# Scores of one pair issued before waiting transposes, copies of the last pair issued at once, a split last accumulator, and another route for the decoded weights

## The chip, the cores and the metric

One core of one Trainium2 chip. The time of a kernel is the device time of one execution in microseconds (us), the median of several executions.

## The reference

Three stages on 4 x 576 = 2304 tokens of width 512 (8 heads of 64):

```python
scores = 0.125 * q @ k.T                       # per batch and head, 576 x 576
scores = where(causal, -1e9, scores + decay)   # decay: differences of cumsum(log(clip(f, 1e-4, 1)))
x = softmax(scores) @ v                        # heads put side by side: 2304 x 512
h = x @ w_in;  x = (h - tanh(h)) @ w_out       # layer 0: 512 -> 2048 -> 512
h = x @ w_in;  x = (h * sigmoid(h)) @ w_out    # layer 1, other weights
```

q, k, v and f arrive as float32, the four weight matrices as float64. The result is float32.

## The kernel before

**Numbers.** TensorE multiplies in a reduced float32 form, so every operand is kept as a high part and the rest (hi and lo), and a product of two operands is three matmuls: hi x hi, hi x lo, lo x hi. The float64 weights have to be decoded first. A `raw` tile holds two 32-bit words of each of 128 x 1024 weights. `wjob` (L191) takes a weight through these steps: `scale` (ACT, L203) rescales the words with the exponent, `shift` (DVE, L207) moves the high word into a tile `wa`, `exponent` (DVE, L211) puts its exponent bits into `wb`, `low` (DVE, L214) turns the low word into a float in `wb`, `join` (DVE, L226) adds the two into `ws`, `sum` (DVE, L230) forms four more blocks of 256 columns in `ws`, and `HI` (ACT, L247) and `LO` (DVE, L249) make the two parts `wh`, `wl` (and `weh`, `wel`) that TensorE reads. A weight is named (q, m): q counts pairs of 128-wide slices of the hidden width, 8 per layer, and m is 0 for w_in and 1 for w_out.

**Attention (0 to about 178 us).** It goes over 16 pairs of heads, each of nine tiles of scores. For pair p the calls `scores(p, u)`, u = 0 to 3, put matmuls into a tile `s`; DVE takes the row minimum (L1328), ACT the exponential (L1336), POOL divides by the sum (L1350). `transposes(p, u)` then turns the tiles p into PSUM tiles `t` (PE, L1362), of which there are three places, and `evac(p, u)` issues the copies of `t` into `ptf` (ACT or DVE, L1407), from which `values` multiplies with v. A list `due` says at which of the tile steps each call is issued; copies are registered one step after their transposes:

```python
later(n0 + k[u], transposes, p, u)
later(n0 + k[u] + 1, evac, p, u)
```

Within a step transposes come before scores. `pt_0` is the tile of the last 64 queries of pair 0, and turning it waits for POOL's L1350 on it.

**Start of layer 0 (about 165 to 263 us).** The first three units (a unit is one set of weights, 4 slices of the hidden width, times one of three blocks of 768 tokens) run from slots written out by hand (PE L475 and L431, ACT L341, L481, L500, L449, DVE L328, L342, L482, L504).

**The joint stage (263 us to the end).** The other 21 units run with two alternating pieces on PE: `h_step` (L656, twelve matmuls of 384 columns, one of seven block products of the first matrix) and `c_step` (L729, eighteen of 256 columns or twelve of 384, one of seven of the second matrix). The products accumulate in four PSUM banks: two `h` and two `a`. Where a partial sum serves two results, ACT copies one bank into the other ("seed", L944 and L1023). `x` collects the results through DVE additions (`gain`, L1031). The order here is not written by hand: `joint` lists tasks with an engine, a cost in steps, what they read and write and a due time, and `planned` (L1123) lays them out engine by engine; each engine then runs its instructions in that order.

**DMA.** Nearly all transfers are issued by SP, in order. An issue that has to wait holds back all behind it. Per unit SP loads seven `xr` tiles (L625, 768 KB). A partial sum of layer 0 that must wait for the next set is put aside: `aside_store` (L673) writes the tile `aside` to DRAM and `aside_load` (L676) brings an earlier one back into the same tile, so the load waits until the store has landed. Loads of `raw` (L164) follow the `low` step of the weight before:

```python
if what[0] == "low":
    raws.pop((q, m))
    wload(q + 1, m)
```

**The end.** In the last unit the seven products of `c_step` come as 1, 5, 6, 2, 7, 3, 4. Products 1, 6, 2, 7 and the last, 4, add into the bank called y, whose sums are also read by other results before product 4 may write it. After product 4 three DVE additions of 256 columns (L1031, `gain(..., d=d)`) go into `x`, and two stores (L801), on ACT's and SP's queue, end the kernel.

Of the kernel before, what the change touches and what calls it, by code (L numbers as in the profile page):

```python
# [48 lines left out]
def forgetting_attention_two_ffn(  # L49
# [104 lines left out]
    raws, wtiles, wjobs = {}, {}, {}  # L154

    def wload(q, m, parts=(0, 1)):
        if q >= 2 * NPR:
            return
        l, c = divmod(2 * q, NFC)
        if (q, m) not in raws:  # L160
            raws[q, m] = rawp.tile([P, 2, DM, 2], U32, tag=f"raw{m}", name=f"raw{q}_{m}")
        for i in parts:
            to = raws[q, m][:, i].rearrange("p n w -> p (n w)")
            nc.sync.dma_start(out=to, in_=(w_in, w_out)[m][l][c + (i if m and q >= 2 * S0 else 1 - i)])  # L164

# [29 lines left out]
    def wjob(q, m, what, part=None):  # L195
# [5 lines left out]
        if what == "scale":  # L201
            high = rd(raws[q, m][:, i, :, 1])
            nc.scalar.activation(high, high, AF.Prelu, scale=2.0 ** -112, alpha=-(2.0 ** 32))  # L203
        elif what == "shift":
            if "a" not in st:
# [21 lines left out]
        elif what == "sum":  # L227
            s = st["s"]
            to, p, op, r = RECIPE[m * (2 - l)][part]
            nc.vector.tensor_tensor(s[:, to], s[:, p], s[:, r], op)  # L230
        elif what in ("hi", "lo"):
            hi, lo = wtile(q, m)
            frm = st["s"][:, 1:8] if m == 0 else st["w"]
            if m:
                hi, lo = (t.rearrange("p (i k) f -> p i (k f)", i=2) for t in (hi, lo))
            c = i if m else (slice(0, 3), slice(3, 7), slice(7, 8))[part]
            frm = st["s"][:, 0:1] if m == 0 and part == 2 else frm[:, c]
            if what == "hi":
                nc.scalar.copy(hi[:, c], frm)
            else:  # L240
                nc.vector.tensor_tensor(lo[:, c], frm, rd(hi[:, c]), ALU.subtract)
        else:
            for to, n, frm in GROUPS[m and l + 1][part]:
                hi, lo = place(q, to) if m else (w[:, to:] for w in wtile(q, 0))
                hi, lo, frm = hi[:, 0:n], lo[:, 0:n], st["s"][:, frm:frm + n]
# [440 lines left out]
    def cbank(u, i):  # L686
# [23 lines left out]
    def c_step(u, k):  # L710
# [7 lines left out]
        for d in range(3 if l else 2):  # L718
            ds = slice(d * P, d * P + P)
            for j, (wh, wl) in enumerate(ws):  # L720
                gh, gl = (t[:, e, j] for e in range(2))
                if l:
                    dst = acc[:, d // 2, 256 * (d % 2):256 * (d % 2) + 256]
# [60 lines left out]

    def csum(u, t, d=None):
        if units[u][0]:
            t = t.rearrange("p b c -> p (b c)")
            return t[:, 0:TB] if d is None else t[:, 256 * d:256 * d + 256]
        return t[:, :, 0:TH]

# [12 lines left out]
    def joint():  # L803
# [15 lines left out]

        W2, N2, basis = dve(TB), act(TB), {}  # L820
        base = {U0: 0}
# [8 lines left out]
        def decode(q, m):  # L830

            l = 2 * q // NFC
            job, raw = (lambda *a: lambda: fill((q, m) + a)), ("raw", m)
            yield "D", 3.5, None, (), (raw,), None
            yield "A", act(DM * 2), job("scale"), (raw,), (raw,), None
            yield "V", 0.33, job("shift"), (raw,), ("wa",), None
            yield "V", 0.33, job("exponent"), ("wa",), ("wb",), None
            yield "V", dve(1024), job("low"), (raw,), ("wb", raw), None
            if m and q // 2 in PLAINSETS:
# [4 lines left out]
                return  # L844
            yield "V", dve(1024), job("join"), ("wa", "wb"), tuple(("ws", k) for k in range(8)), None
            for k, (to, p, op, r) in enumerate(RECIPE[m * (2 - l)]):
                yield "V", dve(256), job("sum", k), (("ws", p), ("ws", r)), (("ws", to),), None
            groups = [0, 1, 2] if m and q // 2 in MIXED else [0, 1]
            behind = m and l and q % 2 and 3 * (q // 2) - 1 in PLAIN and q // 2 not in MIXED
            for g in [1, 3, 4, 5] if behind else groups:  # L850
                cols, key = [("ws", k) for to, n, f in GROUPS[m and l + 1][g] for k in range(f, f + n)], wkeys(q, m, g)
                yield "A", act(256 * len(cols)), job("HI", g), cols, key, g
                yield "V", dve(256 * len(cols)), job("LO", g), cols + key, key, None

        def spread(t0, t1, jobs, since):
# [3 lines left out]
            for e, c, fn, r, w, tag in jobs:  # L859
                if e == "D":  # L860
                    task(t - 6, e, c, fn, r, w)
                    continue
# [53 lines left out]
        for u in range(U0, len(units) + 1):  # L916
# [93 lines left out]
            for k, i in enumerate(csteps(v)):  # L1010
                if plain_:
# [3 lines left out]
                    continue  # L1015
                kd = ("h", v % 2) if last and i in (5, 3) else kz if i in (2, 3, 5) else ky
                n = gop(v, k)
                r = [kd, ("gh", n % 3), ("gl", n % 3)] + [w for j in range(2) for w in (wkeys(q + j, 1, 1) if WAT[l][i] >= 8 else [("w", (q + j) % NSLOT, 1, 10 + WAT[l][i])])]
                when = t0 + k if last else t0 + 2 * k + 1
                task(when, "P", 1, lambda v=v, k=k: c_step(v, k), r, (kd,))  # L1020
# [4 lines left out]
            def gain(when, c, frm, kf, op=PLUS, copies=False, d=None):  # L1025
                to = xs[c] if d is None else xs[c][:, 256 * d:256 * d + 256]
                if copies:
                    task(when, "A", N2, lambda: copy(to, frm), (kf,), (kx[c],), True)
                else:
                    n = W2 if d is None else dve(256)  # L1030
                    task(when, "V", n, lambda: tt_(to, *((frm, to) if op == PLUS else (to, frm)), op), (kf, kx[c]), (kx[c],), True)  # L1031

# [69 lines left out]
            else:  # L1102
# [11 lines left out]
                send(t0 + 6.6, 12)  # L1114
                for d in range(3):
                    gain(t0 + 7.05 + 0.01 * d, 21, csum(v, y, d), ky, d=d)
                    if d:
                        send(t0 + 7.055 + 0.01 * d, 21, slice(0, 2) if d == 1 else slice(2, 3), (nc.scalar, nc.sync)[d - 1])

# [74 lines left out]
    def attention(first):  # L1194
        with ExitStack() as actx:
# [156 lines left out]
            def transposes(p, u):  # L1352
# [277 lines left out]
```

## Time and profile before

| | us |
|---|---|
| median of 3 runs (lowest to highest) | 901.84 (901.59 to 902.15) |
| profiled execution, its time | 901.59 |
| its span, first to last instruction | 899.8 |
| PE busy (6079 matmuls) | 890.6 (99%) |
| DVE busy | 784.7 (87%) |
| ACT busy | 602.2 (67%) |
| POOL busy, all of it before 178 us | 161.2 (18%) |

The granted clock of TensorE is 0.999 of full speed over the span. Rows of the timeline give the start and length of an instruction (or of a run of equal ones, "x4") and, in square brackets, how long its engine stood idle ahead of it and what ended that. Rows of the chain of waits give a start, a length and the engine and line that stood on the path that ended last. "L" is a line of the kernel.

### The profile page before, as it was taken

What the parts mean: (1) busy time and instruction counts of PE and PEld (TensorE: products, weight loads), DVE (VectorE), ACT (ScalarE), POOL (GpSimd) and SP (SyncE); (2) the same over time, 40 slices, a digit from 0 to 9 for tenths busy, and PEclk for the clock granted to TensorE, in tenths of its full rate; (3) what the DMA queues carried; (4) which work ended last, traced back from release to release, by engine and by line L of the source; (5) the groups of instructions that cost most, each with busy time, mean ns of one, the idle gap of its engine ahead of it and who ended that gap; (6) DMA issues with size and microseconds to landing.
All of it is one profiled execution on the core that took longest, in us unless ns stands there. A gap on an engine that the chain in (4) does not pass through costs nothing.

```text
span 899.8 us, 16280 instructions
## 1 busy us (share of the span) xinstructions
PE 890.6 (99%) x6079; PEld 846.1 (94%) x6079; DVE 784.7 (87%) x1321; ACT 602.2 (67%) x1006; POOL 161.2 (18%) x242
## 2 busy tenths in 40 slices
PE   9999999999999999999999999999999999999997
PEld 7777777799999999999999999999999999999997
DVE  7799999798889999998999999997997799776647
ACT  6888888765556666766676678866765666555443
POOL 8999999400000000000000000000000000000000
PEclk9999999999999999999999999999999999999999
DMA  5434533467458677787678665777767566555753
GB/s 166 157 97 149 177 122 97 190 249 279 192 224 304 247 262 245 248 295 273 226 273 290 211 241 202 274 273 266 246 236 264 201 225 231 192 186 179 235 166 123
DMA packets 51103, 196.04 MB, mean 218 GB/s; under 512 B 9744, under 2 KB 15120, under 8 KB 50992
## 3 DMA queue, kind: packets, MB, share of 16 engines
q1 hardware_dynamic: 50744, 194.72, 61.7%
q8 instruction: 48, 0.79, 0.3%
q14 instruction: 31, 0.25, 0.1%
q10 hardware_dynamic: 280, 0.28, 0.1%
HBM read 151.98 MB, written 41.88 MB: 215 GB/s over the span
## 4 chain that ended last, share of the span: by engine, by line
PE 96%; DVE 1%; ACT 1%; POOL 1%; issue 0%; DVEq 0%; POOLq 0%; ACTq 0%
PE h L656 34%; PE a L729 32%; PE a L431 5%; PE t L1362 5%; PE s L1315 5%; PE out_t L1418 5%; PE h L475 4%; PE a L761 2%; PE s L1307 2%; PE h L461 2%; PE out_t L1446 1%; PE out L1418 0%; DVE x L1031 0%; DVE gr L988 0%; PE h L729 0%
## 5 line engine op out<-in xcount | busy, mean ns | idle before, releaser
L656 PE MATMUL h<-xr,wh 128*128 128x384 f32 x1176 | 299.3, 335 | 0.1
L656 PEld LDWEIGHTS h<-xr,wh 128*128 128x128 f32 x1176 | 208.8, 188 | 0.5 <-ACT h L944 0.4
L656 PE MATMUL h<-xr,wl 128*128 128x384 f32 x588 | 196.8, 335 | 0.0
L656 PEld LDWEIGHTS h<-xr,wl 128*128 128x128 f32 x588 | 110.4, 188 | 0.0
L987 ACT CAST gr<-f 128x768 fp32r<-128x768 f32 x104 | 86.8, 838 | 32.5 <-PE a L729 29.9
L988 DVE TENSOR_TENSOR gr<-f,gr 128x768 fp32r<-128x768 f32 x104 | 98.7, 952 | 3.9 <-ACT gr L987 3.9
L729 PE MATMUL a<-wh,gr 128*128 128x256 f32 x516 | 99.2, 282 | 0.0
L1336 ACT ACTIVATE p<-p,mn 128x128 f32<-128x128 f32 (+3 forms) x128 | 71.3, 559 | 18.0 <-DVE mn L1328 15.3
L729 PEld LDWEIGHTS a<-wh,gr 128*128 128x128 f32 x516 | 83.0, 191 | 0.0
L1031 DVE TENSOR_TENSOR x<-a,x 128x768 f32<-128x768 f32 (+1 forms) x64 | 59.3, 929 | 21.4 <-PE a L729 21.1
L729 PE MATMUL a<-weh,gr 128*128 128x256 f32 x384 | 74.1, 283 | 0.3 <-DVE x L1031 0.3
L1350 POOL TENSOR_SCALAR p<-p,sm 128x128 f32<-128x128 f32 (+3 forms) x128 | 72.6, 582 | 7.5 <-DVE sm L1347 6.9
L729 PE MATMUL a<-gr,wh 128*128 128x384 f32 x288 | 73.4, 335 | 0.4 <-DVE gr L988 0.4
L729 PE MATMUL a<-wl,gr 128*128 128x256 f32 x258 | 72.9, 283 | 0.0
L1023 ACT COPY a<-a 128x768 f32<-128x768 f32 x49 | 38.4, 783 | 49.4 <-PE a L729 46.8
L1328 DVE CUSTOM_DVE_ANT_0 p<-s,mask 128x128 f32<-128x128 f32 (+3 forms) x128 | 59.6, 479 | 13.1 <-PE s L1315 13.1
L729 PEld LDWEIGHTS a<-weh,gr 128*128 128x128 f32 x384 | 61.8, 191 | 0.7 <-issue 0.5
L944 ACT COPY h<-h 128x768 f32<-128x768 f32 x42 | 33.0, 785 | 35.0 <-PE h L656 33.8
L729 PE MATMUL a<-gr,weh 128*128 128x384 f32 x216 | 54.9, 334 | 0.0
L729 PE MATMUL a<-wel,gr 128*128 128x256 f32 x192 | 54.2, 282 | 0.0
L1257 POOL TENSOR_TENSOR kqs<-kqraw,kqs 128x288 fp32r<-128x288 f32 (+1 forms) x62 | 53.8, 888 | 1.3
L729 PEld LDWEIGHTS a<-gr,wh 128*128 128x128 f32 x288 | 52.1, 188 | 0.7 <-DVE gr L988 0.7
(169 smaller groups left out, 2072.3 us busy)
## 6 DMA issues: line engine op xcount, KB each, us to landing
xr<-xd SPq DMA_DIRECT2D x126, 768.0 KB
raw<-w_in SPq DMA_DIRECT2D x32, 512.0 KB
raw<-w_out SPq DMA_DIRECT2D x32, 512.0 KB
xd<-xo SPq DMA_DIRECT2D x21, 768.0 KB
xd<-xr SPq DMA_DIRECT2D x21, 768.0 KB
kqraw<-kq SPq DMA_DIRECT2D x16, 608.0 KB
aside<-aside SPq DMA_DIRECT2D x15, 384.0 KB
vraw<-v SPq DMA_DIRECT2D x16, 320.0 KB
```

What stands on the lines that cost most here:

```text
L431: nc.tensor.matmul(dst, w, m, start=first and r == 0, stop=last and r == 2)
L656: nc.tensor.matmul(dst[:, j, 0:TH], w[:, ds], m[:, d], start=i in (1, 5) and d == r == 0, stop=d == 1 and r == 2, skip_group_check=True,)
L729: nc.tensor.matmul(dst, w, m, start=fresh and (l == 0 or d != 1) and j == r == 0, stop=j == 1 and r == 2, skip_group_check=True,)
L987: task(w, "A", N2, lambda g=g, f=frm: copy(g[:, 0], f), (kf,), (("gh", kg),))
L988: task(w + 0.1, "V", W2, lambda g=g, f=frm: tt_(g[:, 1], f, rd(g[:, 0]), MINUS), (kf, ("gh", kg)), (("gl", kg),))
L1031: task(when, "V", n, lambda: tt_(to, *((frm, to) if op == PLUS else (to, frm)), op), (kf, kx[c]), (kx[c],), True)
L1257: eng.tensor_tensor(lo[:, c0:c1], raw[p][:, c0:c1], rd(hi[:, c0:c1]), ALU.subtract)
L1315: nc.tensor.matmul(s[:, h, c:c + n], a[half(h), q], b[half(h), 0:n], start=r == 0, stop=r == 3,)
L1328: nc.vector.tensor_tensor_reduce(out=pt.rearrange("p (g c) -> p g c", g=2) if i == 4 else pt, in0=src, in1=m, op0=ALU.add, op1=ALU.min, sc ...
L1336: nc.scalar.activation(pt, pt, AF.Exp, bias=mn, scale=-1.0, accum_out=sums[:, n // 3 % 5, n % 3, 0:1],)
L1350: nc.gpsimd.tensor_scalar(pt, pt, sm[:, j:j + 1], 1.0, ALU.mult, ALU.mult)
L1362: nc.tensor.transpose(t[:, k], pt[:, c * P:c * P + P], ident)
```

## The change

It has four parts.

1. **Pair 0.** `scores(1, 3)` is issued inside the transposes of pair 0, behind those of tile `p` and ahead of those of `pt_0`. On PE it goes as follows (t: PSUM tiles of transposes, s: of scores, kqs, de and lq: operands of the scores). Before:

```order
L1362 MATMUL t_1_0_413<-ident,p_1_227 128x128 x4
L1362 MATMUL t_1_1_418<-ident,p_1_227 128x128 x2
L1362 MATMUL t_1_1_418<-ident,pt_0_111 128x128
L1362 MATMUL t_1_2_422<-ident,pt_0_111 128x128 x4
L1307 MATMUL s_3_427<-kqs_240,lq_110 128x288 x3
L1307 MATMUL s_3_427<-de_108,lq_110 128x288
L1307 MATMUL s_3_427<-kqs_240,lq_110 128x288 x3
L1307 MATMUL s_3_427<-de_108,lq_110 128x288
L1362 MATMUL t_2_0_446<-ident,p_2_264 128x128 x4
```

Now, on the same engine at the same place:

```order
L1428 MATMUL t_1_0_413<-ident,p_1_227 128x128 x4
L1428 MATMUL t_1_1_418<-ident,p_1_227 128x128 x2
L1373 MATMUL s_3_421<-kqs_240,lq_110 128x288 x3
L1373 MATMUL s_3_421<-de_108,lq_110 128x288
L1373 MATMUL s_3_421<-kqs_240,lq_110 128x288 x3
L1373 MATMUL s_3_421<-de_108,lq_110 128x288
L1428 MATMUL t_1_1_418<-ident,pt_0_111 128x128
L1428 MATMUL t_1_2_431<-ident,pt_0_111 128x128 x4
L1428 MATMUL t_2_0_446<-ident,p_2_264 128x128 x4
```

The eight matmuls of the scores have moved ahead of the five transposes of `pt_0`.

2. **The last pair.** Its copies are issued in the step of their transposes. On ACT, before, from the rescaling of a weight on (t_1_0, t_2_0, t_3_0: transposes of the last pair; the rows between them belong to the first unit of layer 0):

```order
L203 ACTIVATE raw_1_2257<-raw_1_2257 128x1024
L239 CAST wh_0_2897<-ws_0_2444 128x256
L481 ACTIVATE t_0_0_2906<-h_0_0_1_2917 128x384
L1407 COPY ptf_105<-t_1_0_2924 128x2x2x128
L341 CAST xo_6_2958<-xt_0_1_2915 128x768
L500 CAST gh_0_0_2970<-t_0_0_2906 128x768
L1407 COPY ptf_105<-t_2_0_2944 128x2x2x128
```

Now:

```order
L235 ACTIVATE raw_1_2257<-raw_1_2257 128x1024
L286 CAST wh_0_2899<-ws_0_2444 128x256
L1476 COPY ptf_105<-t_1_0_2924 128x2x2x128
L535 ACTIVATE t_0_0_2908<-h_0_0_1_2917 128x384
L1476 COPY ptf_105<-t_2_0_2946 128x2x2x128
L395 CAST xo_6_2960<-xt_0_1_2915 128x768
L554 CAST gh_0_0_2972<-t_0_0_2908 128x768
```

The copy of t_1_0 has moved ahead of one instruction and that of t_2_0 ahead of two; on DVE copies move in the same way.

3. **The end.** Product 4 of the last unit goes into the other `a` bank (its first 512 columns) and an `h` bank (the last 256). ACT copies y there first. The three additions of 256 columns become one of 512 and one of 256.

4. **Weights.** For the 25 weights in `ADDED` (w_out from q = 3 on, w_in from q = 4 on) the shifted high words go straight into `ws`, or, for every other weight, their first four blocks into `wa`; the low words are worked out in place in `raw` and added to the high words where these lie. For the three in `BYDMA` the addition is a transfer that accumulates, issued from POOL. HI and LO pieces are cut where a weight lies in both places. Loads of `raw` are tasks of their own for the planner, six steps ahead of the first use. What this does to SP's order, for instance near unit 13, before (xd: DRAM copies of the xr tiles):

```order
L625 DMA xr_4816<-xd_1_6_3257 128x1536
L625 DMA xr_4853<-xd_1_3_3184 128x1536
L164 DMA raw_1_4858<-w_out 128x1024 x2
L673 DMA aside_3_4862<-aside 128x768
L676 DMA aside<-aside_1_4355 128x768
L625 DMA xr_4897<-xd_1_7_3338 128x1536
```

Now:

```order
L679 DMA xr_4805<-xd_1_6_3257 128x1536
L679 DMA xr_4840<-xd_1_3_3184 128x1536
L727 DMA aside_3_4847<-aside 128x768
L730 DMA aside<-aside_1_4349 128x768
L196 DMA raw_0_4850<-w_in 128x1024 x2
L679 DMA xr_4883<-xd_1_7_3338 128x1536
```

Another load of `raw` stands here, and it stands behind the load that waits for the store. On ACT the rescaling of that `raw_0` stands between two copies of banks, as another one did before:

```order
L1004 ACTIVATE f_3811<-h_3810 128x768
L1051 CAST gr_3818<-f_0_3820 128x768
L1008 COPY h_3810<-h_3809 128x2x384
L235 ACTIVATE raw_0_4850<-raw_0_4850 128x1024
L1088 COPY a_3802<-a_3795 128x2x384
L1051 CAST gr_3819<-f_3813 128x768
```

Where now the freshly loaded raw_0_4850 stands, there stood before a `raw` that had been loaded 50 us earlier.

The diff, cut:

```diff
+    ADDED = [(2 * S0 + 1, 1)]
+    for g in range(S0, 2 * NSET - 1):
+        o = 2 * g + 1
+        ADDED += [(o, 1), (o + 1, 0), (o + 1, 1), (o + 2, 0)] if g >= NSET else [(o + 1, 0), (o, 1), (o + 1, 1), (o + 2, 0)]
+    ADDED = list(dict.fromkeys(ADDED + [(2 * NPR - 1, 1)]))
+    BYDMA = {(NPR, 0), (NPR + 1, 0), (NPR + 1, 1)}
...
+    def block(q, m, k, n=1):
+        if (q, m) not in ADDED:
+            return wjobs[q, m]["s"][:, k:k + n]
+        if k + n <= 4 and ADDED.index((q, m)) % 2 == 0:
+            return tmp("wa", [P, 4, 256])[:, k:k + n]
+        return tmp("ws", [P, 8, 256])[:, k:k + n]
...
+        elif (q, m) in ADDED and what in ("shift", "exponent", "low", "join"):
+            high, factor = row(block(q, m, 0, 4)), row(tmp("wb", [P, 4, 256]))
+            words = raws[q, m].rearrange("p i n w -> p (i n) w")
+            low = rd(raws[q, m][:, 0].rearrange("p n w -> p (n w)"))
+            if what == "shift":
+                nc.vector.tensor_scalar(high.bitcast(U32), words[:, :, 1], 3, None, ALU.logical_shift_left)
...
+            elif what == "low":
+                nc.vector.scalar_tensor_tensor(low, words[:, :, 0], 2.0 ** -52, factor, ALU.mult, ALU.mult)
+            elif (q, m) in BYDMA:
+                nc.gpsimd.dma_start(out=high, in_=low, accum_op=ALU.add, max_dma_last_dim=8 * DM)
+            else:
+                nc.vector.tensor_tensor(high, high, low, ALU.add)
...
-        if what[0] == "low":
+        if what[0] == ("join" if (q, m) in ADDED else "low"):
             raws.pop((q, m))
-            wload(q + 1, m)
+            if (q, m) not in ADDED:
+                wload(q + 1, m)
...
+        if u == LASTU and i == 4:
+            return (z, z, chain(u)[1]), False
...
-            yield "D", 3.5, None, (), (raw,), None
+            yield "D", 3.5, (lambda: wload(q, m)) if (q - 1, m) in ADDED else None, (), (raw,), "load"
...
-                for d in range(3):
-                    gain(t0 + 7.05 + 0.01 * d, 21, csum(v, y, d), ky, d=d)
...
+                for d, (c, t, kt) in enumerate(((slice(0, 512), z, kz), (slice(512, 768), chain(v)[1], ("h", 1 - v % 2)))):
+                    to, part = xs[21][:, c], csum(v, t)[:, c]
+                    n = c.stop - c.start
+                    task(t0 + 5.04 + 0.01 * d, "A", act(n), lambda to=part, frm=ys[:, c]: copy(to, frm), (ky,), (kt,), True)
+                    task(t0 + 7.05 + 0.01 * d, "V", dve(n), lambda to=to, frm=part: tt_(to, frm, to, PLUS), (kt, kx[21]), (kx[21],), True)
...
+                    if both and p == 0:
+                        scores(1, 3)
...
-                    if p + u:
+                    if p + u and (p, u) != (1, 3):
                         later(n0 + k, scores, p, u)
...
-                    later(n0 + k[u] + 1, evac, p, u)
+                    later(n0 + k[u] + (p < NP - 1), evac, p, u)
```

## Rows read from the trace of the kernel before

**Rows 1.** The page: busy time and share by engine.

```profile
PE 890.6 (99%) x6079; PEld 846.1 (94%) x6079; DVE 784.7 (87%) x1321; ACT 602.2 (67%) x1006; POOL 161.2 (18%) x242
```

**Rows 2.** Waits of PE: total us, times, longest us.

```profile
PE t L1362 <- POOL pt L1350: 0.9, 1, 0.9
PE t L1362 <- ACT ptf L1407: 0.9, 2, 0.6
```

**Rows 3.** Chain of waits, 19 to 28 us: start, length, what.

```profile
23.11 0.75 POOL pt L1350
...
24.68 1.07 PE s L1307 x8
25.74 0.87 PE t L1362 x8
```

**Rows 4.** Timeline of POOL, 22 to 26.7 us.

```profile
23.82 2.46 POOL L1257 TENSOR_TENSOR kqs<-kqraw,kqs 128x288 fp32r<-128x288 f32 x3
```

**Rows 5.** Timeline of PE, 173 to 178 us, the last pair's transposes.

```profile
173.46 0.60 PE L1362 MATMUL t<-ident,p 128*128 128x128 f32 x4
174.68 0.66 PE L1362 MATMUL t<-ident,p 128*128 128x128 f32 x4 [0.62 <-ACT ptf L1407]
...
177.43 0.33 PE L1362 MATMUL t<-ident,pt 128*128 128x128 f32 x1 [0.30 <-ACT ptf L1407]
```

**Rows 6.** Timeline of ACT, 172 to 180 us.

```profile
173.16 0.39 ACT L239 CAST wh<-ws 128x256 fp32r<-128x256 f32 x1
...
174.04 0.58 ACT L1407 COPY ptf<-t 128x512 f32<-128x512 f32 x1
```

**Rows 7.** Timelines of ACT and PE near 207 us.

```profile
206.70 0.79 ACT L449 COPY x<-a 128x768 f32<-128x768 f32 x1
...
207.71 0.34 PE L431 MATMUL a<-gh,wh 128*128 128x384 f32 x1
```

**Rows 8.** Timelines of PE and DVE at the end.

```profile
892.79 0.36 PE L729 MATMUL a<-weh,gr 128*128 128x256 f32 x1 [0.29 <-DVE x L1031]
...
893.75 0.96 DVE L1113 TENSOR_TENSOR x<-x 128x768 f32<-128x768 f32 x1
895.22 1.09 DVE L1031 TENSOR_TENSOR x<-a,x 128x256 f32<-128x256 f32 x3 [0.52 <-PE a L729]
```

**Rows 9.** Groups by shape, DVE: busy us, mean ns | idle before.

```profile
L226 DVE TENSOR_TENSOR ws<-wa,wb 128x1024 f32<-128x1024 f32 x28 | 34.2, 1221 | 0.4
L211 DVE TENSOR_SCALAR wb<-wa 128x1024 uint32<-128x1024 uint32 x29 | 20.0, 689 | 0.3
```

**Rows 10.** Timeline of SP's queue, around 378 and 407 us: issues.

```profile
377.77 0.32 SPq L625 DMA_DIRECT2D xr<-xd  x1
...
407.26 0.42 SPq L673 DMA_DIRECT2D aside<-aside  x1
412.60 0.32 SPq L676 DMA_DIRECT2D aside<-aside  x1
```

**Rows 11.** Timelines of SP and ACT, 255 to 270 us: a load and its first use.

```profile
263.35 0.81 SPq L164 DMA_DIRECT2D raw<-w_out  x2
...
268.26 1.14 ACT L203 ACTIVATE raw<-raw 128x1024 f32<-128x1024 f32 x1 [0.76 <-DMA raw<-w_out]
```

**Rows 12.** Transfers, 405 to 414 us: rate in 40 slices.

```profile
GB/s 437 437 382 410 437 300 0 0 0 0 0 0 137 218 0 82 0 82 55 382 355 382 382 382 437 410 341 328 437 410 314 109 73 0 0 0 0 0 205 191
```

**Rows 13.** Timelines of ACT and PE, 385 to 391 us.

```profile
388.18 0.78 ACT L1023 COPY a<-a 128x768 f32<-128x768 f32 x1 [0.22 <-PE a L729]
...
390.06 0.51 PE L729 MATMUL a<-gr,wh 128*128 128x384 f32 x2
```

**Rows 14.** Timelines of SP and PE, 484 to 506 us.

```profile
490.47 0.42 SPq L673 DMA_DIRECT2D aside<-aside  x1
497.37 0.32 SPq L676 DMA_DIRECT2D aside<-aside  x1
...
504.46 0.51 PE L656 MATMUL h<-xr,wh 128*128 128x384 f32 x2
```

More of the change, by code (lines that the diff above doesn't have):

```diff
@@ L154, in forgetting_attention_two_ffn, with tmp, row @@
     raws, wtiles, wjobs = {}, {}, {}
+    ADDED = [(2 * S0 + 1, 1)]
[4 more added lines that the diff above has]
+    BYDMA = {(NPR, 0), (NPR + 1, 0), (NPR + 1, 1)}
+    lasting = {}
+    def tmp(tag, shape, dtype=F32):
+        if tag not in lasting:
+            lasting[tag] = wtmp.tile(shape, dtype, tag=tag, name=f"{tag}_")
+        return lasting[tag]
+    def block(q, m, k, n=1):
[4 more added lines that the diff above has]
+        return tmp("ws", [P, 8, 256])[:, k:k + n]
+    def row(t):
+        return t.rearrange("p k f -> p (k f)")
     def wload(q, m, parts=(0, 1)):
@@ L162, in wload @@
         for i in parts:
-            to = raws[q, m][:, i].rearrange("p n w -> p (n w)")
-            nc.sync.dma_start(out=to, in_=(w_in, w_out)[m][l][c + (i if m and q >= 2 * S0 else 1 - i)])
+            to, frm = row(raws[q, m][:, i]), (w_in, w_out)[m][l][c + (i if m and q >= 2 * S0 else 1 - i)]
+            if m and (q, m) in ADDED:
+                to = raws[q, m].rearrange("p i n w -> p (i n w)").rearrange("p (k i z) -> p k i z", k=2, i=2)[:, :, i]
+                frm = frm.rearrange("p (k z) -> p k z", k=2)
+            nc.sync.dma_start(out=to, in_=frm)
     PLUS, MINUS = ALU.add, ALU.subtract
@@ L242, in wjob @@
         else:
-            for to, n, frm in GROUPS[m and l + 1][part]:
+            pieces = [(to, n, frm) for to, n, frm in GROUPS[m and l + 1][part]]
+            if (q, m) in ADDED and ADDED.index((q, m)) % 2 == 0:
+                pieces = [
+                    piece for to, n, frm in pieces
+                    for piece in ([(to, 4 - frm, frm), (to + 4 - frm, n - 4 + frm, 4)] if frm < 4 < frm + n else [(to, n, frm)])
+                ]
+            for to, n, frm in pieces:
                 hi, lo = place(q, to) if m else (w[:, to:] for w in wtile(q, 0))
-                hi, lo, frm = hi[:, 0:n], lo[:, 0:n], st["s"][:, frm:frm + n]
+                hi, lo, frm = hi[:, 0:n], lo[:, 0:n], block(q, m, frm, n)
                 if what == "HI":
@@ L783, in quarter, with csum @@
         return xblock(b, 2 - c // 10, c % 10 - 1)
[L785 to L789, printed above, removed]
+    def csum(u, t):
+        return t.rearrange("p b c -> p (b c)")[:, 0:TB] if units[u][0] else t[:, :, 0:TH]
     def hsum(t):
@@ L833, in decode @@
             job, raw = (lambda *a: lambda: fill((q, m) + a)), ("raw", m)
-            yield "D", 3.5, None, (), (raw,), None
+            yield "D", 3.5, (lambda: wload(q, m)) if (q - 1, m) in ADDED else None, (), (raw,), "load"
             yield "A", act(DM * 2), job("scale"), (raw,), (raw,), None
-            yield "V", 0.33, job("shift"), (raw,), ("wa",), None
-            yield "V", 0.33, job("exponent"), ("wa",), ("wb",), None
-            yield "V", dve(1024), job("low"), (raw,), ("wb", raw), None
+            added = (q, m) in ADDED
+            own = added and ADDED.index((q, m)) % 2 == 0
+            blk = [("wa" if own and k < 4 else "ws", k) for k in range(8)]
+            wa = blk[0:4] if added else [("wa", k) for k in range(4)]
+            if added and ADDED.index((q, m)) == 0:
+                wa = wa + [("ws", k) for k in range(8)]
+            yield "V", 0.33, job("shift"), (raw,), wa, None
+            wa = wa[0:4]
+            yield "V", 0.33, job("exponent"), wa, ("wb",), None
+            yield "V", dve(1024), job("low"), (raw, "wb"), ("wb", raw), None
             if m and q // 2 in PLAINSETS:
@@ L844, in decode @@
                 return
-            yield "V", dve(1024), job("join"), ("wa", "wb"), tuple(("ws", k) for k in range(8)), None
+            if added:
+                yield *(("D", ADDING) if (q, m) in BYDMA else ("V", dve(1024))), job("join"), [raw] + wa, wa, None
+            else:
+                yield "V", dve(1024), job("join"), ["wb"] + wa, tuple(("ws", k) for k in range(8)), None
             for k, (to, p, op, r) in enumerate(RECIPE[m * (2 - l)]):
-                yield "V", dve(256), job("sum", k), (("ws", p), ("ws", r)), (("ws", to),), None
+                yield "V", dve(256), job("sum", k), (blk[p], blk[r]), (blk[to],), None
             groups = [0, 1, 2] if m and q // 2 in MIXED else [0, 1]
@@ L850, in decode @@
             for g in [1, 3, 4, 5] if behind else groups:
-                cols, key = [("ws", k) for to, n, f in GROUPS[m and l + 1][g] for k in range(f, f + n)], wkeys(q, m, g)
+                cols, key = [blk[k] for to, n, f in GROUPS[m and l + 1][g] for k in range(f, f + n)], wkeys(q, m, g)
                 yield "A", act(256 * len(cols)), job("HI", g), cols, key, g
@@ L1016, in joint, with gain @@
                 kd = ("h", v % 2) if last and i in (5, 3) else kz if i in (2, 3, 5) else ky
+                kds = (kz, ("h", 1 - v % 2)) if last and i == 4 else (kd,)
                 n = gop(v, k)
[L1018 removed]
+                r = [*kds, ("gh", n % 3), ("gl", n % 3)] + [w for j in range(2) for w in (wkeys(q + j, 1, 1) if WAT[l][i] >= 8 else [("w", (q + j) % NSLOT, 1, 10 + WAT[l][i])])]
                 when = t0 + k if last else t0 + 2 * k + 1
[L1020 removed]
+                task(when, "P", 1, lambda v=v, k=k: c_step(v, k), r, kds)
             def seed(when):
                 task(when, "A", N2, lambda to=zs, frm=ys: copy(to, frm), (ky,), (kz,), True)
[L1025 to L1026 removed]
+            def gain(when, c, frm, kf, op=PLUS, copies=False):
+                to = xs[c]
                 if copies:
```

18 lines of the change are left out of this document (9 added, 9 removed).

## The prediction

> **What bounds the kernel now.** I read the page first, then the waits of PE, then the chain of waits, then timelines where either shows another engine than PE. The page has PE busy for 890.6 us of a span of 899.8 [rows 1], and the number of matmuls is not changed. So only two things can move the time: idle time of PE (with the stretch after its last matmul), and new waits that the moved instructions give it. DVE, busy for 784.7 us, is no bound as long as PE doesn't wait for it. The waits of PE name two places that the change touches in attention, 0.9 us behind POOL's L1350 and 0.9 us behind copies on ACT [rows 2]; the timeline of the end adds 0.29 us behind a DVE addition and what follows PE's end [rows 8]. The reader should see how little that is: about 2.1 us of idle time, a quarter of a per cent, and the rest of PE's row is matmul behind matmul. Any new wait of a microsecond or two takes it back.
>
> **Pair 0.** POOL divides pt_0 from 23.11 to 23.86 [rows 3], and PE stands idle 0.9 us for it [rows 2]; the eight score matmuls then take 1.07 us from 24.68 on [rows 3]. Put into the gap, they start at about 22.97 (0.9 before PE goes on, just after 23.86) and end at 24.04, after POOL. The wait goes, and everything behind is 0.9 us earlier. What is late next: the scores of pair 2 follow the eight transposes at 25.74 [rows 3] and read the low parts that POOL makes in three pieces from 23.82 to 26.28 [rows 4]. PE would be there at 25.74 + 0.87 - 0.9 = 25.7; the second piece ends near 25.5, the third at 26.28. If the third were needed at once, 0.6 us would go back. I take 0.9 gained, bounds 0.3 and 1.0.
>
> **Last pair.** t_2_1 waits for the place that the copy of t_1_0 frees. Before it four transposes start at 173.46 [rows 5]; at 0.87/8 = 0.109 each [rows 3] the next four could follow at 173.90, and they start at 174.68, so 0.78 is lost. In the new order the copy stands right behind the cast that starts at 173.16 and takes 0.39: it ends near 173.55 + 0.58 = 174.13 instead of 174.62 [rows 6], and t_2_1 starts near 174.2: 0.5 gained. t_3_1 waits 0.30 [rows 5] for the copy of t_2_0, which moves ahead of a cast and an activation; that goes, with some 0.1 of refilling, and t_3_0 just ahead of it, held by a DVE copy that moves likewise, gives about 0.2 by my estimate. Sum 1.1. Part is given back: DVE and ACT have the same work and don't get earlier by as much as PE. At 207.71 PE reads behind a bank copy on ACT that ends at 207.49, a cover of 0.2 [rows 7]. If the copy came at its old time, 0.9 of the 1.1 would be lost there; if it moves along, nothing. DVE and ACT stand idle between, so I take 0.3 back: net 0.8, bounds 0 and 1.3.
>
> **The end.** Product 4 no longer writes what the additions read, so the wait of 0.29 [rows 8] and, as I estimate, 0.1 of refilling go: PE ends 0.4 earlier, near 894.8. Then DVE is the bound. It works on until 893.75 + 0.96 = 894.71 [rows 8] and then has the addition of 512 columns. That one is not in the trace of before; between 0.36 (a third of the 1.09 for three of 256) and 0.96 (one of 768) [rows 8] I take the middle, 0.65. With 0.36 for the last 256, DVE ends at about 895.7 instead of 896.3. Gain 0.6, bounds 0.2 and 0.8. The two copies of y on ACT stand where ACT has nothing else to do, and only PE's last product waits for them; y is complete some two microseconds ahead.
>
> **Weights.** No PE wait of before stands behind a weight. 25 joins stay about as long (1.22 us [rows 9]), three of them leave DVE: 3.7 us of DVE that PE does not wait for, worth 0. The cut HI and LO pieces add some 40 short instructions on engines with room: 0. An accumulating transfer is not in the trace. From its issue to the first sum that reads it DVE's new order has over twenty instructions of mostly 768 columns, at 0.96 each [rows 8] some 20 us of cover. A store of 384 KB takes 5.3 to 6.9 us to land [rows 10, 14]; twice that for more bytes and a read of the target still lies within. I take 0, bounds -0.2 and +1 for what it takes from other transfers.
>
> **The loads that moved.** This is what I expect to cost. In the new SP order, raw_0_4850 stands behind the aside load, and that waits for its store. The store follows the xr issue at 377.77 by about 0.4; the same sequence near 407 has 412.60 - 407.26 = 5.3 from the store to the load [rows 10]. So the load is issued at 378.15 + 5.3 = 383.5, the raws from 383.9 on. A pair of raws with nothing ahead had its scaling start 268.26 - 263.35 = 4.9 after its issue [rows 11]; the 0.39 MB of the aside load ahead of them take 0.9 at the best rate seen, 437 GB/s [rows 12], less the 0.4 by which its issue leads. So the scaling starts at 389.3. Behind it on ACT stand the bank copy that PE reads at 390.06, and two casts for PE. With 1.14 [rows 11] and 0.78 [rows 13] the scaling has to start by 388.1. PE waits 1.2 us. If nothing of the load delays the raws it is 0.7; if the store takes the 6.9 us of 490.47 to 497.37 [rows 14] it is 2.8. Only if the store came well below all that I saw would it be 0.
>
> A second place: before 504.46 two raws now go ahead of the xr that h reads there. Load, raws and xr are 2.23 MB, 5.1 us at 437 GB/s, and the fixed part is 4.9 - 2.4 = 2.5 (the pair of raws, less its 1.05 MB at that rate). With the aside load at 490.47 + 5.3 = 495.8 the xr is there at 503.4, 1.0 ahead; with the load where it is now, 497.37 [rows 14], at 505.0, 0.6 late; at 300 GB/s from there at 507.3, 2.9 late. I take 0.4.
>
> The sum: -0.9 - 0.8 - 0.6 + 0 + 1.2 + 0.4 = -0.7, from the profiled execution's 901.59 (its span of 899.8 and 1.8 around it) to 900.9. That execution is 0.25 below the median of the runs, 901.84, so the forecast is 0.1% below the median. Differences within 0.2%, 1.8 us, are what a measurement of this kernel cannot tell from none: faster means below 900.04, slower above 903.64.
>
> **Rivals.** *The loads come in time.* Then the gains of 2.3 stay whole: 899.3. For it: the best rate holds and the store has no other traffic behind it; ACT's scaling needs 1.2 us less than I found. Against it: 5.3 is the smallest gap I saw between store and load. A fit in the Trainium skill (SBUF — State Buffer, The DMA setup-cost knee) makes a transfer 2 us and its bytes at 436 GB/s. By it the raws alone need 4.4, where the trace has 4.9, and xr with store together 4.7, where it has 5.7; the wait would be about 0.3 and the time 900.0, on the edge of this rival. Chance 0.25.
>
> *The edits of attention are swallowed.* The third low piece of pair 2 is needed at once, and the 207.71 copy stays where it was: -0.3 - 0.2 - 0.6 + 1.6 = +0.5: 902.1. For it: the small cover [rows 7]. Against it: idle time of the other engines between. Chance 0.1.
>
> *SP's queue costs more than everything saves* (slower). If the store takes 6.9 us each time and transfers go at 300 GB/s, the first place costs 2.8 + 1.1 = 3.9 and the second 2.9, so -2.3 + 6.8: 906.1. It is slower from 4.4 us of waits on. For it: nothing else can be issued while SP stands at the aside load, and this repeats in four units of layer 0. Against it: the xr loads behind were early enough so far, PE waiting for none. Chance 0.16, with times from 903.7 on.
>
> *The accumulating transfers are late* (slower). DVE, in order, would stand at the first sum, and all its additions for PE behind it. At 25 us from issue to landing, 5 above the cover, three times: 900.9 + 15 = 915.9. It decides from about 21 us on. Against it: the 5 to 7 us of plain transfers. Chance 0.04. The Trainium skill (DMA: Bandwidth & Descriptors, SWDGE vs HWDGE vs iDMA) says that an accumulating transfer is always prepared by GpSimd in software, which writes its lists in SBUF, and that DVE's two-port modes shut it out meanwhile. DVE's L211 takes 689 ns for 1024 columns where an addition takes 1221 [rows 9], so such a mode is in use here; no row of before has a transfer of that kind, and by the page alone I would double this chance.
>
> **How the numbers follow.** Forecast 0.45 (of it 0.07 below 900.04), loads in time 0.25, swallowed 0.1, SP 0.16, accumulation 0.04. Faster 0.25 + 0.07 = 0.32; same 0.38 + 0.1 = 0.48; slower 0.2. The range goes from 898.9, with no wait and the gains near their upper ends, to 904.5 for the smaller half of the SP rival. The likeliest case by itself covers 899.8 to 902.5.
>
> **What would show it.** In the profile after: PE without idle time at 22.97, and none behind POOL's L1257; no gap over 0.3 at 174 to 178, and a short one near 206.5; product 4 starting with no wait, and DVE, not PE, last in the chain. Near 388 PE should wait for L1088 behind L235, whose wait ends with a transfer of raw, 1 to 2 us; near 502 PE may wait for xr. I am wrong if PE waits for a weight, if DVE stands at L277 for an accumulating transfer, or if L235 finds its raw in place.

## The result, and the profile after

The changed kernel takes 907.93 us (median of 6 runs, 905.31 to 909.52) against 901.64 us for the kernel before in the same sessions: a ratio of 1.0065, 95% interval 1.0055 to 1.0076. It is slower by some 6 us, where 0.7 us less was forecast, and above the top of the range (904.5). The profiled execution took 909.52 us with a span of 907.7, 7.9 more than before; it is the longest of the six, 1.6 above the median, and the places below are read from it.

The waits of PE in the profile after (total us, times, longest us) answer to [rows 2]:

```profile
PE h L710 <- ACT a L1088: 3.2, 1, 3.2
PE a L786 <- ACT a L1088: 2.1, 1, 2.1
PE out_t L1515 <- POOL de L1507: 1.8, 1, 1.8
PE s L1373 <- DMA lq<-kqs: 1.1, 1, 1.1
PE h L710 <- DMA xr<-xd: 0.7, 1, 0.7
PE s L1381 <- DMA de<-x: 0.6, 1, 0.6
```

The two waits of before, for POOL and for the copies, are gone; the 1.8 at the start is in both. Two waits behind a bank copy on ACT (L1088, "seed"), one for lq, one for xr and a short one at 10.7 us for de are new.

The first of the two long ones, near 391 us, on the timelines of SP, ACT and PE; it answers to [rows 10, 13]:

```profile
376.90 0.42 SPq L727 DMA_DIRECT2D aside<-aside  x1
382.32 0.32 SPq L730 DMA_DIRECT2D aside<-aside  x1
382.68 0.91 SPq L196 DMA_DIRECT2D raw<-w_in  x2
...
389.24 1.11 ACT L235 ACTIVATE raw<-raw 128x1024 f32<-128x1024 f32 x1 [3.61 <-DMA raw<-w_in]
390.25 0.79 ACT L1088 COPY a<-a 128x768 f32<-128x768 f32 x1
...
391.10 0.61 PE L786 MATMUL a<-gr,wh 128*128 128x384 f32 x2 [2.12 <-ACT a L1088]
...
391.81 0.84 PE L786 MATMUL a<-gr,wh 128*128 128x384 f32 x2
```

The store is issued at 376.90, the load waits for it until 382.32, the raws go out behind it and arrive at 389.2; ACT stands idle 3.6 us, and PE 2.1. The rows of PE behind show something else: two matmuls of 384 columns take 0.64 us to the next matmul (391.81 to 392.45), where before they took 0.35 (390.06 to 390.41). The granted clock (third number from the right) by stretches (start:end, length, then busy time and number of instructions of PE, PE's loads, DVE, ACT and POOL, the clock, the DMA share and GB/s):

```profile
391.10:395.00 3.90, 3.90 (x13) 3.90 (x14) 2.85 (x7) 2.51 (x5) 0.00 (x0) 0.56 0.67 275
395.00:400.00 5.00, 5.00 (x30) 5.00 (x30) 4.87 (x6) 3.98 (x6) 0.00 (x0) 1.00 0.37 100
...
424.80:428.00 3.20, 3.18 (x18) 3.18 (x19) 3.20 (x4) 3.10 (x4) 0.00 (x0) 1.00 1.02 400
...
511.50:515.00 3.50, 3.49 (x12) 3.50 (x13) 1.59 (x2) 0.63 (x1) 0.00 (x0) 0.58 0.58 241
```

For some 3 us behind each long wait the clock is at its lower level, 1.2 of 2.4 GHz (0.56 and 0.58 are means over stretches that hold a little of the upper level). Behind the wait of 0.7 us for xr (424.8 on) it stays at 1.00. The six runs of the changed kernel have mean clocks of 0.994 to 0.999, and the shortest, 905.31 us, has 0.999 as the kernel before has: how often the clock falls differs from run to run, and without its fall the time is still 3.7 us longer.

The second long wait, on the chain of waits (start, length, what); it answers to [rows 14]:

```profile
494.22 7.03 DMA aside<-aside
501.27 0.32 SPq L730
...
501.64 0.55 SPq L196
...
502.24 7.25 DMA raw<-w_out
...
509.57 0.04 ACT raw L235
...
510.58 0.80 ACT a L1088
```

It is the same sequence: store, load, raw, rescaling, bank copy. Store and raw take 7 us each here, and not the xr, which I had feared for, but the raw is late.

Where the time went, by the start of the same matmul in both traces (plus is later):

| place | forecast | profile |
|---|---|---|
| pair 0 | -0.9 | +0.4 |
| last pair | -0.8 | -1.6 |
| near 391 | +1.2 | +4.0: wait 2.2, lower clock 1.6, rest 0.2 |
| near 424, xr late | 0 | +1.0: wait 0.8, small ones |
| near 511 | +0.4 | +4.8: wait 3.4, lower clock 1.4 |
| near 532, a wait of 0.43 for `gr` gone, and small ones | 0 | -0.9 |
| end | -0.6 | +0.3: PE -0.5, behind PE's end +0.8 |
| sum | -0.7 | +8.0 (the terms are rounded; span: +7.9) |

### The profile page after: what moved, and what is told of

It is laid out like the page before. It is cut to its first block, busy times and chain, and to the rows that moved or that the text cites. A ratio compares the mean times of both kernels' runs of the same rounds, so it can differ in the third digit from the quotient of the medians.

```text
span 907.7 us, 16304 instructions
## 1 busy us (share of the span) xinstructions
PE 892.8 (98%) x6079; PEld 848.7 (94%) x6079; DVE 781.1 (86%) x1330; ACT 603.4 (66%) x1021; POOL 165.9 (18%) x245
## 4 chain that ended last, share of the span: by engine, by line
PE 87%; DVE 6%; DMA 5%; ACT 1%; issue 1%; SPq 0%; DVEq 0%; ACTq 0%
PE h L710 30%; PE a L786 28%; PE t L1428 5%; PE a L485 5%; PE s L1381 5%; PE out_t L1487 5%; PE h L529 4%; PE a L818 2%; PE s L1373 2%; PE h L515 1%; DMA aside<-aside 1%; DVE gr L1052 1%; DMA raw<-w_out 1%; DMA xr<-xd 1%; DVE x L1095 1%
## 5 line engine op out<-in xcount | busy, mean ns | idle before, releaser
L1051 ACT CAST gr<-f 128x768 fp32r<-128x768 f32 x104 | 87.1, 839 | 32.6 <-PE a L786 29.4
L1095 DVE TENSOR_TENSOR x<-a,x 128x768 f32<-128x768 f32 x61 | 58.1, 953 | 26.4 <-PE a L786 25.8
L1088 ACT COPY a<-a 128x768 f32<-128x768 f32 x49 | 38.4, 784 | 43.7 <-PE a L786 43.6
L248 POOL DMA_DIRECT2D wa__3920<-raw x2 | 1.9, 942 | 286.8 <-DVE raw L246 286.8
```

What stands on the lines that cost most here:

```text
L1051: task(w, "A", N2, lambda g=g, f=frm: copy(g[:, 0], f), (kf,), (("gh", kg),))
L1095: task(when, "V", W2, lambda: tt_(to, *((frm, to) if op == PLUS else (to, frm)), op), (kf, kx[c]), (kx[c],), True)
```

## The experiments

**1. Loads at the join.** In `fill` the next raw is loaded right behind a join, and the planner's own load tasks are gone:

```diff
-            if (q, m) not in ADDED:
-                wload(q + 1, m)
+            wload(q + 1, m)
```

> The changed kernel with one thing undone: a raw tile is loaded again right behind the join of the weight before it, so that each load is issued some 20 us or more ahead of its use. Theory (the cost lies in raw loads that stand behind the wait of the aside load on SP, and in ACT's in-order queue behind them): the waits of 2.1 us near 391 and 3.2 us near 511, and the stretches at the lower clock behind them, go; time 899.5 to 901.5. Rival (the decode itself, with its in-place low words, accumulating transfers and short pieces, is what costs): time stays at 906 or more.

913.35 us (912.45 to 915.07), ratio 1.0132 (1.0119 to 1.0146): a miss in the total. The waits near 391 and 511 did go (the matmul at 390.06 of before starts 1.7 earlier, like all around it), but PE waits 0.8 and 1.2 us for xr near 421 and 451, and 5.6 us near 552. The chain there:

```profile
542.26 0.88 DVE x L1094
543.14 0.36 SPq L196
...
544.20 0.03 SPq L691
...
544.26 6.58 DMA xd<-xr
...
550.95 0.07 ACT xr L975
...
551.68 0.80 ACT a L1110
```

Now the raw waits on SP for DVE, and a store of an xr tile stands behind it; ACT needs that tile, and PE needs ACT's next copy. By this chain SP's order was still at fault, with another victim. Behind this wait PE works at the lower clock for 4.1 us and loses 2.0 more (columns as in the stretches above):

```profile
552.50:556.60 4.10, 4.07 (x13) 4.07 (x14) 3.32 (x4) 3.60 (x5) 0.00 (x0) 0.50 0.39 159
```

**2. The three other edits alone.** The kernel before with parts 1 to 3 of the change, no weight edits.

> The kernel before with the edits of pair 0, the last pair and the end, and none of the weight edits. Theory from the profile of the changed kernel: +0.3 at pair 0 (the scores wait for the transfer of lq instead), -1.6 in the last pair, +0.3 at the end (PE 0.5 earlier, but DVE 0.8 longer behind it): 900.6, no wait near 391 or 511. Rival (these edits move DVE and ACT so that they also cost in the joint stage): 902 or more.

900.14 us (899.64 to 900.53), ratio 0.9983 (0.9974 to 0.9992). A little below the 900.6 expected: no new wait in the joint stage (the one of 0.43 for `gr` is in the kernel before too), last pair -1.6, pair 0 without gain (PE waits 0.7 for lq).

**3. The weights alone.** The changed kernel with parts 1 to 3 undone.

> The changed kernel without the edits of pair 0, the last pair and the end: only the weights' new route. Theory: about 8.5 us above the kernel before in a profile like that of the changed kernel, 907 to 910 in the median, with waits of PE behind L1088 near 391 and 511. Rival (the waits come from PE being earlier after the last pair's edit): 903 or less.

909.54 us (906.09 to 911.30), ratio 1.0075 (1.0057 to 1.0094). As expected: PE's earlier arrival is not the cause; the waits near 391 and 511 are 3.2 and 2.0 us here, the second behind a cast on ACT (L1051). The clock falls at both (0.57 in the stretch from 513.4 to 517.4, behind the second), and each loses 1.7 more.

**4. Joins on DVE.** `BYDMA = set()`.

> The changed kernel with the three accumulating transfers replaced by additions on DVE. Theory: the late raws come from SP's order, so the wait near 391 stays at about 2 us and that near 511 at 2 to 3; time 906 to 908.5. Rival (the accumulating transfers fill the DMA engines and make the store near 494 and the raws behind it late): the wait near 511 shrinks to below 1 us and the time falls to 904 or less.

912.54 us (909.95 to 913.78), ratio 1.0117 (1.0104 to 1.0131): slower than with the transfers, so both numbers missed, the rival's by its sign. Its planner orders DVE anew, and raw loads wait on SP for DVE (its additions stand ahead of L196 on the chain); PE waits behind L1088 three times (2.57, 3.81 and 0.45 us), and 2.25 us for xr near 516. The first two take the clock down, by 1.7 and 1.6 more; the last does not, though it is longer than waits of 1.98 and 2.04 that do in runs 3 and 6 (the wait, then the stretch behind it):

```profile
515.89 0.59 PE L710 MATMUL h<-xr,wh 128*128 128x384 f32 x2 [2.25 <-DMA xr<-xd]
...
515.90:519.00 3.10, 3.10 (x18) 3.10 (x19) 2.69 (x5) 1.27 (x2) 0.00 (x0) 1.00 0.46 191
```

The accumulating transfers themselves took 5.7 to 7.1 us from issue to landing in the changed kernel, and DVE waited for none.

**5. Loads at the join, from POOL.** As 1, with `nc.gpsimd` in place of `nc.sync` for these loads.

> As the first experiment (a raw tile is loaded again right behind the join of the weight before), but these loads are issued from POOL, which does nothing else in the joint stage, so neither an aside load nor a raw tile that is not free yet holds back SP's queue. Theory (the cost is SP's in-order queue: raws behind the aside load, or xr and xd transfers behind a raw that waits for its tile): the waits near 391, 421, 450, 511 and 545 all go; time 899.3 to 901. Rival (raws on any queue delay the xr transfers on the shared engines, or the decode order itself costs): waits of 1 us and more stay, 903 or more.

903.79 us (903.05 to 904.87), ratio 1.0024 (1.0015 to 1.0032): a miss, where the rival had 903 or more. All waits for raws and xr up to 511 went; 3.2 us are lost between 537 and 562, where the chain runs through DVE's making of xr tiles. Loading at the join gives the planner another order there, so this run does not separate order from queue; run 11 does.

**6. Waits of a chosen length.** The kernel before, one bank copy in each of four units repeated (same values):

```diff
-                task(when, "A", N2, lambda to=zs, frm=ys: copy(to, frm), (ky,), (kz,), True)
+                more = {14: 2, 16: 3, 18: 4, 20: 6}.get(v, 0) if when < t0 + 5 else 0
+                task(when, "A", N2, lambda to=zs, frm=ys: [copy(to, frm) for _ in range(1 + more)], (ky,), (kz,), True)
```

> The kernel before with one bank copy on ACT repeated 2, 3, 4 and 6 times more in four units of layer 1 (the same values are written again), so that PE has to wait there. By the rows of before PE has about 2.08 - 0.9 = 1.2 us of cover; each copy takes 0.73 to the next. Waits expected: 0.3, 1.0, 1.7 and 3.2 us. Theory (a wait of PE of some 2 us or more is followed by about 3.6 us at the lower clock, 1.5 us more lost): the first two cost only themselves, the last about 4.7, the third in between; sum 8 to 10 us, 909.5 to 912. Rival (the slow matmuls behind the waits belong to something else, such as the transfers running then): each costs its wait and no more, 6.2 us, 908.

912.69 us (912.19 to 913.18), ratio 1.0119 (1.0103 to 1.0134). The four waits on PE's timeline:

```profile
619.63 0.38 PE L729 MATMUL a<-wh,gr 128*128 128x256 f32 x1 [0.47 <-ACT a L1024]
680.44 0.38 PE L729 MATMUL a<-wh,gr 128*128 128x256 f32 x1 [1.23 <-ACT a L1024]
742.01 0.39 PE L729 MATMUL a<-wh,gr 128*128 128x256 f32 x1 [2.04 <-ACT a L1024]
806.80 0.39 PE L729 MATMUL a<-wh,gr 128*128 128x256 f32 x1 [3.67 <-ACT a L1024]
```

and the clock around them (columns as above):

```profile
619.00:623.00 4.00, 3.53 (x26) 3.37 (x26) 3.56 (x6) 2.91 (x5) 0.00 (x0) 1.00 0.92 324
679.00:683.00 4.00, 2.77 (x22) 2.56 (x21) 2.24 (x5) 3.05 (x5) 0.00 (x0) 1.00 0.75 263
741.50:745.50 4.00, 3.48 (x19) 3.49 (x20) 2.23 (x4) 2.91 (x6) 0.00 (x0) 0.68 0.43 171
806.50:810.50 4.00, 3.70 (x20) 3.70 (x21) 2.18 (x5) 2.14 (x4) 0.00 (x0) 0.66 0.03 12
```

By the starts of the matmuls behind, against before, the waits of 0.47 and 1.23 cost 0.7 and 1.5 in all, those of 2.04 and 3.67 cost 3.8 and 5.5: the longer two lose 1.5 to 1.6 more, at a clock of 0.66 and 0.68 with a DMA share of 0.43 and 0.03. So the slow matmuls belong to the wait, not to transfers. The sum is 11.5, the span 11.6 longer; the time lies a little above the 909.5 to 912 expected, because the waits are 0.2 to 0.5 longer and the third costs as much of the clock as the last.

**7. The end, first try.** The kernel before with the last pair's edit and the new end, the second copy of y due later, by its time alone. In this kernel the copy stands behind the matmuls that should add to it, so the products of the last 256 columns are lost.

> The kernel before with the edit of the last pair, and that of the end with the second bank copy of y issued behind both DVE additions that read y. Theory: -1.6 in the last pair; at the end PE ends 0.5 earlier and DVE, which no longer alternates with ACT in reading y, ends about 0.6 earlier than before: 899.3 to 899.5. Rival (the end is bound by the last transfers, whose length is what it is, or the second copy now holds PE): 900 or more.

899.66 us (899.43 to 900.56), ratio 0.9977 (0.9968 to 0.9986). Run 9 is the same with the order mended.

**8. Aside loads from POOL.** The changed kernel with one word changed:

```diff
-        nc.sync.dma_start(out=to, in_=aside[b])
+        nc.gpsimd.dma_start(out=to, in_=aside[b])
```

> The changed kernel with one thing different: the loads that bring an aside tile back are issued from POOL's queue, so that SP does not stand there until the store has landed. The raws are then issued right behind the store, about 5 us earlier. Theory (SP's wait at the aside load makes the raws late): no wait of PE behind a raw near 391 and 511, none for xr near 421; what stays is +0.3 at pair 0, -1.6 in the last pair, +0.3 at the end and perhaps -0.6 near 532: 899.8 to 901.5. Rival (the raws come late from the transfers ahead of them in the queue, whatever SP waits for): the wait near 391 shrinks by less than half, 904 or more.

904.15 us (901.94 to 907.16), ratio 1.0024 (1.0014 to 1.0034). Near 391 PE does not wait, so what SP waits for does decide; 3.8 us of the loss are gone. But it is not all: on POOL the accumulating transfers now stand behind aside loads and take 7.8 to 12.1 us; DVE stands 3.5 and 1.9 us for two of them, and waits of PE of 0.2 to 1.3 us appear at four places of the joint stage, the longest near 538 behind a rescaling again. A miss in the total: the time is the rival's, though the wait near 391 went as the theory had it. Whether the late accumulating transfers make the new waits of PE was not tried.

**9. The end mended.** The kernel before with the last pair's edit and the new end, with the second copy of y made to follow the DVE subtraction that reads y:

```diff
-                    task(t0 + 5.04 + 0.01 * d, "A", act(n), ..., (ky,), (kt,), True)
+                    task(t0 + (5.04, 5.95)[d], "A", act(n), ..., (ky, kx[12]), (kt,), True)
```

> The kernel before with the last pair's edit, and that of the end with the second bank copy of y issued behind the DVE subtraction that reads y, so that ACT and DVE no longer take turns. Theory: -1.6 in the last pair, PE's end 0.5 earlier, DVE's end 0.6 earlier than before: 899.3 to 899.6. Rival (the last transfers set the end, or PE's last third now waits for the later copy): 900.0 or more.

899.71 us (899.65 to 899.75), ratio 0.9974 (0.9964 to 0.9985): a little above the expected 899.3 to 899.6, by what the last stores take back (see the end, below).

**10. The same with the edit of pair 0.**

> The one above with the edit of pair 0 added. Theory (the scores now wait for the transfer of lq, which takes back what the wait for POOL cost): within 0.4 us of the one above. Rival (on most executions lq lands in time): 0.6 to 0.9 faster.

899.61 us (899.13 to 899.93), ratio 0.9972 (0.9961 to 0.9983): 0.1 from run 9, as expected; PE waits 1.0 for lq in its profile instead of 1.0 for POOL.

**11. The same order, another queue.** The changed kernel with the loads of raw for the added weights issued from POOL where it issues them from SP. PE, DVE and ACT have the same instructions in the same order.

```diff
-            nc.sync.dma_start(out=to, in_=frm)
+            (nc.gpsimd if (q - 1, m) in ADDED else nc.sync).dma_start(out=to, in_=frm)
```

> The changed kernel with nothing different but the queue that issues the loads of raw for the added weights: POOL's instead of SP's. The instructions of PE, DVE and ACT stand in the same order as in the changed kernel. Theory (raws are late because SP stands at the aside load ahead of them, and xr late because SP's raws go ahead of them): the waits near 391 and 511 and the lower clock behind them go, that near 421 too; 900 to 902. Rival (the new order of DVE and ACT in the joint stage costs by itself, and the late raws only show it): waits of 2 us and more in sum stay, 903 or more.

900.28 us (899.69 to 905.76), ratio 0.9991 (0.9980 to 1.0002). All waits in the joint stage are gone. PE's waits, and the timelines of POOL and ACT ahead of 391 us:

```profile
PE out_t L1515 <- POOL de L1507: 1.8, 1, 1.8
PE s L1373 <- DMA lq<-kqs: 0.9, 1, 0.9
PE s L1381 <- DMA de<-x: 0.5, 1, 0.5
```

```profile
363.45 1.10 POOL L196 DMA_DIRECT2D raw<-w_in  x2
...
385.37 1.20 ACT L235 ACTIVATE raw<-raw 128x1024 f32<-128x1024 f32 x1
386.76 0.78 ACT L1088 COPY a<-a 128x768 f32<-128x768 f32 x1 [0.19 <-PE a L786]
```

The raw is on its way 19 us earlier, and ACT does not wait for it. With nothing else changed this gives back 7.6 of the 907.93 us. A few of its 12 runs reach 902 to 906; which wait comes back in those was not seen.

**12. The same with the end of run 9.**

> The one above with the end of the ninth experiment (second bank copy of y behind the subtraction that reads y). Theory: 0.5 to 1 us faster than the one above; if that one comes to 900.5, this one is level with the ninth experiment's 899.7. Rival (the weights' new route leaves waits in the joint stage on any queue): 902 or more, and the end's gain of 0.5 to 1 still seen against the one above.

899.58 us (899.03 to 901.99), ratio 0.9981 (0.9971 to 0.9992): 0.7 better than run 11 and level with runs 9 and 10. So the weights' route, freed of the waits, is worth nothing that can be measured. No kernel here is faster than runs 9, 10 and 12, 2.1 to 2.2 us below the kernel before.

## Why the prediction was wrong, step by step

**The loads that moved: right mechanism, wrong size, and the step that failed.** "PE waits 1.2 us" near 391 was the sequence that the trace shows: store to load 5.4 us (5.3 forecast), raws from issue to rescaling 6.6 (5.4 forecast), rescaling and copy as forecast. The wait became 2.1: the raws behind the aside load were mis-sized. Three things were left out of the term, which was 1.6 in the sum and measured 9.8. First, what a wait does to the clock: I priced idle time alone, and the two long waits cost 1.6 and 1.4 us more at 1.2 GHz, which run 6 shows without any late transfer. The Trainium skill has this as a rule (TensorE: Matmul & The Clock Gate, HAM oscillation — how this bites in real kernels: a wait for a transfer can throw PE back to half its clock, and the next work starts slow). The traces agree that a wait can do this, not that each does: no drop after waits of 0.47, 0.7, 1.23 and, in run 4, 2.25 us, a drop after 1.98, 2.04, 2.1 and all of 2.57 and more. What else decides near 2 us is open. Second, the second place: I followed the xr ahead of h and took 0.4, though the same `scale` on ACT stands there ahead of a bank copy as at the first place; it cost 4.8, of it 3.4 wait. This is the largest miss: without the clock's 3.0 us the profiled execution would still be near 906.5, above the range. Third, the smaller one for xr near 424.

The rival that I gave 0.16, SP's queue, is what happened, nearly at its price (906.1 against 907.93), in part by luck: its 6.8 us of waits are near the 6.4 measured, but it had the second place wait for xr, nothing for the clock, and gains of 2.3 where 1.8 came. It was held down by "the xr loads behind were early enough so far", which was true of the kernel before and beside the point: the late tile was raw, and what was blocked was ACT, which takes its instructions in order.

Two sums of the rivals are off, without bearing on this. In the one that the loads come in time, what is given there (1.0 less from store to load, 0.5 less for the raws) leaves 0.3 us to spare of a wait of 1.2, not a wait of 0.3, and so 899.7 and not 900.0. In that of SP's queue, the 300 GB/s are counted for the raws at the first place, not for the load ahead of them, some 0.4 us.

**Pair 0: wrong.** "Put into the gap, they start at about 22.97" took the scores' operands for granted. The chain after, which answers to [rows 3]:

```profile
16.94 2.05 SPq L1328
...
19.04 5.00 DMA lq<-kqs
...
24.17 1.29 PE s L1373 x8
```

lq, the last queries of pair 1, is itself brought by a transfer that lands at 24.04. Before, the scores came behind that, at 24.68 on the chain [rows 3]. The wait for POOL was exchanged for a wait on a transfer; runs 9 and 10 put the difference at 0.1 us. What I had bounded instead, POOL's low parts for pair 2, cost nothing.

**Last pair: right, undersized.** PE after, which answers to [rows 5]:

```profile
173.85 1.04 PE L1428 MATMUL t<-ident,p 128*128 128x128 f32 x8
...
175.80 0.71 PE L1428 MATMUL t<-ident,pt 128*128 128x128 f32 x5
```

Eight and five transposes run through without a wait; the gain is 1.6, and the give-back near 207 did not come: the copy there moved along with PE. The three steps gave 0.8, 0.3 and 0.5 by the starts of the transposes, where 0.5, 0.2 and 0.4 were summed.

**The end: the missed wait.** PE's part (-0.5) was right. DVE was to run on without a gap. ACT and DVE after, which answer to [rows 8]:

```profile
897.97 0.57 ACT L1182 COPY a<-a 128x512 f32<-128x512 f32 x1 [1.39 <-PE a L786]
899.56 0.36 ACT L1182 COPY h<-a 128x256 f32<-128x256 f32 x1 [1.02 <-DVE x L1095]
...
898.57 0.95 DVE L1095 TENSOR_TENSOR x<-x,a 128x768 f32<-128x768 f32 x1
899.95 0.96 DVE L1095 TENSOR_TENSOR x<-a,x 128x768 f32<-128x768 f32 x1 [0.42 <-ACT h L1182]
```

All four read the bank y, and they take turns, though reads change nothing: ACT, DVE, ACT, DVE. DVE stands 0.42 for ACT's second copy. The Trainium skill says why a program must do so (PSUM — Partial Sum Buffer, PSUM bank collisions raise a hardware error: two engines may not touch one bank at a time, reads included); here it is seen as waits in the program. I had called the copies free because ACT was. In run 9 the second copy comes behind both of DVE's reads (DVE 889.42 and 890.29, ACT 891.28) and DVE goes on without that gap. Of the +0.8 behind PE's end in the changed kernel, 0.3 is DVE; 0.5 lies behind DVE's last addition, in the last stores (4.0 us to the end of the span instead of 3.5). The same is seen in every kernel with the new end (3.8 to 4.0 us) and in none with the old (3.5 in runs 3 and 6), so that run 9, whose DVE ends 0.7 earlier there, gains only 0.3. With the new end the store ahead of the last two is issued 0.6 us before them instead of 1.3; whether that is the cause was not tried. The forecast had put this stretch at no change without a reason.

**Weights: right.** The forecast of 0 for the DVE time that leaves the path, and for the accumulating transfers, held: run 12 is level with runs 9 and 10, and DVE waits for none of the accumulating transfers in the profile after, where they land 5.7 to 7.1 us after their issue.

## What to carry to other kernels

When loads move in a queue that issues in order, follow each of them to the first instruction that needs it and then to everything behind that instruction on its engine; a load behind another transfer's completion starts late by that whole transfer, 5 to 7 us here. Price a wait of a busy TensorE with what its clock may do next: each wait of 2 to 3.8 us here but one cost 1.4 to 1.7 us more, and one of 5.6 us cost 2.0. A load whose place in time matters little for the data belongs on a queue where nothing else waits (run 11: one line, 7.6 us); but what already stands in that queue gets later, as the accumulating transfers did in run 8.

## What was not expected of the hardware

TensorE at full load kept its clock through waits of 0.47, 0.7 and 1.23 us and lost it at waits of 1.98 and 2.04 us already (granted clock 0.68 in the stretch shown for the latter), yet kept it through one of 2.25 us in run 4 (1.00). A wait of 3.67 us cost no more beyond its length than one of 2.04. In run 11 the loads of raw, most of them from POOL, landed in 3.9 to 10.7 us (median 6.6), beside a DVE busy for 87% of the span and without a wait of PE in the joint stage of the profiled execution.
